# Cosine attention and a two-layer network: two and a half more group products by seven half-size products, another order of loads, one list of all operations

## The chip, the core and the metric

The kernel runs on one core of a Trainium2 chip. The core has engines with instruction queues of their own, each worked in order: TensorE (PE, with its weight loads PEld), VectorE (DVE), ScalarE (ACT), GpSimd (POOL), and SyncE (SP), which here issues nearly all DMA transfers. Matrix products are written into PSUM, eight banks of 128 partitions with 512 float32 each; operands lie in SBUF. The metric is the device time of one execution in microseconds. Before the change it is 274.62 us (median of 3 runs, 274.36 to 274.9).

## The reference

```python
batch, n_heads, seq, head_dim = (8, 8, 576, 64)          # q, k, v
theta = np.pi / 2.0 * pos / S
def phi(x, c, s):
    r = np.maximum(x, 0.0)
    return np.concatenate([r * c, r * s], axis=-1)       # 64 -> 128 features
q_p, k_p = phi(q, cos_w, sin_w), phi(k, cos_w, sin_w)
kv = np.einsum('bhsf,bhsd->bhfd', k_p, v)
z = np.sum(k_p, axis=2)
num = np.einsum('bhsf,bhfd->bhsd', q_p, kv)
den = np.einsum('bhsf,bhf->bhs', q_p, z)[..., None] + 1e-06
x = (num / den)                      # tokens 8 * 576 = 4608, d_model 8 * 64 = 512
h = x @ w_in                         # 512 -> 2048
g = np.maximum(0.01 * h, h)
out = g @ w_out                      # 2048 -> 512
```

Linear attention with cosine weights, for each batch and head, and then a two-layer network over all tokens. Nearly all the arithmetic is in the two products with `w_in` (called FFN1 here) and `w_out` (FFN2).

## The kernel before, in words

The tokens are worked in nine groups of 512: group g below 8 is the first 512 tokens of batch g, and group 8 is the last 64 tokens of all eight batches. For each batch the stages are these.

- Loads of q, k and v (float32) into stage buffers, and their preparation: `q_prep` and `k_token` (or `k_pair` for the first two batches) write relu(x) times the cosine and sine columns as float16, `v_pairs` casts v and leaves a column of ones beside it, which makes the sum z.
- `kv_sum`: 72 small matmuls over the keys of a batch, the key sum, copied by ACT into `kv`.
- q is transposed, by TensorE (`q_transpose`) for the first two batches and by DMA afterwards. `num` multiplies it with kv into PSUM, `divide` (three DVE instructions: add, reciprocal, multiply) writes x, and x is transposed into xT: by TensorE for groups 0 to 2, by DMA from group 3 on.
- FFN1 of the group: w_in has 16 tiles of 128 columns ("f-tiles", m) and 4 chunks of 128 rows (c). As whole products this is 16 x 4 matmuls of 512 token columns (`ffn1`), each pair of f-tiles followed by one ACT activation over 1024 columns into g.
- FFN2 of the group: 4 token tiles x 16 f-tiles, matmuls of 512 columns (`ffn2_mm`), or by seven products.

"By seven half-size products" means that a product of two matrices cut into 2 x 2 quarters is made of seven products of quarters (or of sums of quarters) instead of eight. For FFN1, `ffn1s` makes it in four units u with seven products n, each of four matmuls of 256 columns; `ffn1e` does what lies between: three copies in or out of PSUM (`b`, `s`, `u`), two additions (`y`, `z`), four half-size activations (`a`, `c`, `e`, `d`). The sums of quarters are made once for the weights (`w1_sum`) and once per group for x (`x_sum`). For FFN2, `ffn2s` makes the seven products, `weight_sum` the sums of the weights, `g_sum` those of g, and three partial results t1, t2, t3 and four results (`result`) follow on ACT and DVE.

In the kernel before, FFN1 is made whole for groups 0, 1 and 2 and by seven from group 3 on (`F7 = 3`, line 53); FFN2 is made whole for group 0 and by seven from group 1 on (`G7 = 1`, line 52).

The order of the work is written out by hand up to line 1014: the loads in lines 174 to 187 and 905 to 917, the attention of the first two batches, FFN1 of group 0, FFN2 of group 0 woven with the preparation of batch 1, and the first half of FFN1 of group 1. From there on the table `TUNE` (line 1020) gives the order of TensorE's units (strings in `O`) and, for every other operation, a place among them and an engine; `weave` merges the two. Each engine's queue gets its instructions in the order in which Python issues them; the dependences between engines become semaphore waits. `idle` matmuls (lines 194 to 199 and later) on a blank tile stand at places in the start where TensorE waits for data.

Stage buffers: four rotating ones, and beside them `ext` and `wext`, which hold chunks of w_in, of the fourth quarter of w_out, of v of batch 1 and of k of batches 1 and 3, until the sums of the seven products need that space.

## Time and profile before

| | |
|---|---|
| median of 3 runs | 274.62 us (274.36 to 274.9) |
| profiled execution, first to last instruction | 273.1 us |
| TensorE busy | 265.3 us |
| VectorE, ScalarE, GpSimd busy | 204.8, 179.2, 130.3 us |
| bytes moved by DMA | 57.07 MB |
| granted TensorE clock | 1.00 in every stretch |

The profile is of one execution; the page gives its own time as the span of 273.1 us from the first to the last instruction, 1.5 us less than the median of the runs. Two views of it, and how they are read. The page cuts the span into 40 slices of 6.83 us; a digit is the busy share of an engine in a slice, in tenths:

```profile
PE   8899999999999999999999999999999999999993
DVE  4850596677876796996989798897789957757852
ACT  7756547577985878898778776776744575565500
POOL 2586002992779456998695879742330004000000
DMA  6999999999899899869999996794565051111214
```

The groups of instructions have a line of the kernel, an engine, an operation, output and input with their shapes and a count; then the busy time and the mean duration of one in ns, and the idle time of that engine just before them with what ended it. A group of matmuls has a mean that is longer than the distance from one to the next, because matmuls are pipelined; the distance is read from a chain or a timeline, as length divided by count.

### The profile page before, as it was taken

How to read it: one execution, taken by the hardware profiler on the slowest of the kernel's cores; microseconds unless marked ns; L12 is line 12 of the kernel's file. 1: busy time of each engine (PE TensorE's matmuls, PEld its weight loads, DVE VectorE, ACT ScalarE, POOL GpSimd, SP SyncE). 2: the span in 40 equal slices, each digit the busy share in tenths (PEclk: the TensorE clock that was granted, in tenths of full speed). 3: DMA queues.
4: the chain of work that ended last, by engine and by line, in shares of the span. 5: the costliest groups of instructions: out<-in, count | busy, mean ns of one | idle time of the engine just before them, and what ended most of it. 6: DMA issues, size and time to landing. Idle time of an engine off the chain costs nothing.

```text
span 273.1 us, 7061 instructions
## 1 busy us (share of the span) xinstructions
PE 265.3 (97%) x2877; PEld 218.6 (80%) x2877; DVE 204.8 (75%) x419; ACT 179.2 (66%) x311; POOL 130.3 (48%) x104
## 2 busy tenths in 40 slices
PE   8899999999999999999999999999999999999993
PEld 3575555556885589999999999899999899999983
DVE  4850596677876796996989798897789957757852
ACT  7756547577985878898778776776744575565500
POOL 2586002992779456998695879742330004000000
PEclk9999999999999999999999999999999999999999
DMA  6999999999899899869999996794565051111214
GB/s 212 382 392 411 382 399 371 374 278 253 247 191 320 205 186 353 265 120 264 208 238 206 244 388 105 125 211 93 119 154 118 2 115 65 54 41 35 83 38 116
DMA packets 75120, 57.07 MB, mean 209 GB/s; under 512 B 47312, under 2 KB 63696, under 8 KB 74704
## 3 DMA queue, kind: packets, MB, share of 16 engines
q1 hardware_dynamic: 74480, 56.11, 74.6%
q10 hardware_dynamic: 608, 0.52, 0.6%
q8 instruction: 22, 0.36, 0.5%
q14 instruction: 10, 0.08, 0.1%
HBM read 36.70 MB, written 9.44 MB: 169 GB/s over the span
## 4 chain that ended last, share of the span: by engine, by line
PE 90%; DMA 3%; DVE 2%; POOL 1%; SPq 1%; issue 1%; ACT 1%; DVEq 0%
PE ps L759 34%; PE ps_f L642 27%; PE ps_h L490 15%; PE ps_o L516 5%; PE ps_kv L330 4%; DMA kst<-in_k_dram 3%; PE ps_num L416 3%; PE ps_f L759 1%; POOL kp L257 1%; PE ps_qt L402 1%; PE ps_xth L468 1%; PE ps_x L393 0%; SPq L135 0%; ACT g L500 0%; SPq L121 0%
## 5 line engine op out<-in xcount | busy, mean ns | idle before, releaser
L759 PEld LDWEIGHTS <-g 128*128 128x128 f16 x640 | 61.8, 98 | 7.5 <-ACT g L500 0.6
L759 PE MATMUL ps<-w,g 128*128 128x256 f16 x496 | 65.3, 273 | 0.4 <-ACT g L500 0.4
L669 ACT ACTIVATE g<-ps_f 128x512 f16<-128x512 f32 x72 | 41.9, 597 | 20.0 <-PE ps_f L642 10.3
L490 PE MATMUL ps_h<-xT,w 128*128 128x512 f16 (+1 forms) x208 | 43.5, 363 | 0.1
L642 PEld LDWEIGHTS <-w 128*128 128x128 f16 x384 | 41.6, 114 | 1.1 <-issue 0.3
L642 PE MATMUL ps_f<-xT,w 128*128 128x256 f16 x288 | 42.1, 273 | 0.2 <-DVE u L265 0.2
L490 PEld LDWEIGHTS <-w 128*128 128x128 f16 x208 | 22.8, 114 | 16.4
L500 ACT ACTIVATE g<-ps_h 128x1024 f16<-128x1024 f32 x24 | 24.1, 1023 | 13.1 <-PE ps_h L490 13.1
L759 PE MATMUL ps<-T,ext 128*128 128x256 f16 x240 | 32.4, 273 | 0.0
L257 POOL TENSOR_SCALAR kp<-kst,cos_t 128x256 f16<-128x256 f32 (+1 forms) x23 | 29.8, 1302 | 5.2 <-DMA kst<-in_k_dram 3.2
L642 PEld LDWEIGHTS <-wext 128*128 128x128 f16 x288 | 31.2, 113 | 0.5
L759 PEld LDWEIGHTS <-ext 128*128 128x128 f16 x256 | 24.8, 98 | 2.5
L257 POOL TENSOR_SCALAR qp<-qst,cos_t 128x512 f16<-128x512 f32 (+1 forms) x10 | 19.5, 1951 | 9.1 <-DMA qst<-in_q_dram 5.0
L257 POOL TENSOR_SCALAR kp<-kst,sin_t 128x256 f16<-128x256 f32 x15 | 20.2, 1348 | 4.9 <-PE ps_kv L330 2.7
L642 PE MATMUL ps_f<-X,wext 128*128 128x256 f16 x144 | 21.5, 273 | 0.0
L542 DVE TENSOR_TENSOR osb<-ps,ext 128x512 f32<-128x512 f32 x23 | 15.8, 688 | 7.4 <-PE ps L759 6.3
L542 DVE TENSOR_TENSOR ps_f<-ps_f,u 128x512 f32<-128x512 f32 x24 | 16.6, 694 | 5.6 <-PE ps_f L642 3.3
L432 DVE TENSOR_TENSOR xs<-ps_num,rden 128x512 f16<-128x512 f32 x28 | 19.4, 691 | 1.0
L669 ACT ACTIVATE g<-y 128x512 f16<-128x512 f32 x24 | 15.2, 632 | 6.9 <-DVE y L542 6.6
L257 POOL TENSOR_SCALAR qp<-qst,sin_t 128x512 f16<-128x512 f32 (+1 forms) x10 | 19.5, 1951 | 0.0
L542 DVE TENSOR_TENSOR ext<-g 128x512 f16<-128x512 f16 (+1 forms) x24 | 13.8, 576 | 5.1 <-ACT g L500 3.5
L542 DVE TENSOR_TENSOR y<-ps_f,s 128x512 f32<-128x512 f32 x24 | 16.4, 683 | 1.4 <-PE ps_f L642 1.3
(120 smaller groups left out, 455.9 us busy)
## 6 DMA issues: line engine op xcount, KB each, us to landing
out_dram<-osb SPq DMA_DIRECT2D x32, 256.0 KB, 2.6
qst<-in_q_dram SPq DMA_DIRECT2D x7, 1024.0 KB, 9.1
kst<-in_k_dram SPq DMA_DIRECT2D x5, 1152.0 KB, 7.6
vst<-in_v_dram SPq DMA_DIRECT2D x5, 1152.0 KB, 9.5
w2st<-in_moe_w_out_dram SPq DMA_DIRECT2D x3, 1024.0 KB, 14.1
vst<-in_v_dram SPq DMA_DIRECT2D x4, 576.0 KB, 6.4
ext<-in_moe_w_in_dram SPq DMA_DIRECT2D x4, 512.0 KB, 10.1
kst<-in_k_dram SPq DMA_DIRECT2D x2, 576.0 KB, 7.3
```

Source lines behind the costliest of these rows:

```text
L257: eng.tensor_scalar(out=o, in0=i, scalar1=0.0, scalar2=col, op0=ALU.max, op1=ALU.mult)
L330: nc.tensor.matmul(ps[:, o, (c - lo) * NE : (c - lo + 1) * NE], lhsT=st["kp", b][sl, c, j, :], rhs=vm[sl, c, j, :], start=(j == 0), stop=( ...
L402: nc.tensor.transpose(ps[:, h, :], qp[:, h, :], ident)
L416: nc.tensor.matmul(ps[lo:hi, h // 4, (h % 4) * NE : (h % 4 + 1) * NE], lhsT=qpT[:, h, lo:hi], rhs=kv[b][:, h, :],)
L432: nc.vector.tensor_tensor(out=xs, in0=ps[:, :, 0 : 4 * NE].rearrange("p a (b e) -> p a b e", e=NE)[:, :, :, 0:D], in1=rden.rearrange("p (a ...
L490: nc.tensor.matmul(ps[:, m % 2, lo:hi], lhsT=w1[m // 4, c][0][:, w1[m // 4, c][1], m % 4 : 512 : 4], rhs=xT[:, lo // P : hi // P, c, :], s ...
L500: nc.scalar.activation(st["g", g][:, m - 1 : m + 1, :], ps, AF.Lrelu)
L516: nc.tensor.matmul(st["ps_o", g, tt], lhsT=st["g", g][:, m, tt * P : (tt + 1) * P], rhs=w2[:, m, :], start=(m == 0), stop=(m == NFT - 1),)
L542: eng.tensor_tensor(out=o, in0=a, in1=b, op=op)
L642: nc.tensor.matmul(ps[:, mi * HT : (mi + 1) * HT], lhsT=a[:, c, 2 * r0 + mi : 512 : 4], rhs=b[:, c], start=(n in (1, 5) and mi == 0 and c ...
L669: nc.scalar.activation(st["g", g][:, m : m + 2, r * HT : (r + 1) * HT], {"a": A, "c": y22, "e": E, "d": B_}[e].rearrange("p (m t) -> p m t ...
L759: nc.tensor.matmul(ps[:, tt], lhsT=a[:, i, tt * P : (tt + 1) * P], rhs=b[:, i], start=(first and i == 0), stop=(i == NPR - 1 and (apart or ...
```

## The change

Three things change, and the code is rewritten around them.

1. FFN1 of groups 1 and 2 is made by seven products too (group 0 stays whole), and of FFN2 of group 0 the second eight f-tiles: its first eight are 4 x 8 matmuls of 512 columns (`E`), copied into the output tile `osb` (`ec`); the second eight are half of the seven products (`F0.n.tt.1`, four matmuls each). Their results are added to what lies in `osb` (`r0.n`), and so are t3, t1 and t2 (`d0.5`, `d0.4`, `d0.3`).
2. The loads come in another order. In the start: the first half of k, the second and then the first half of q, the second half of k, the first half of v, one chunk of w_in, the second half of v, the other chunks, with the first half of k of batch 1 ahead of the last of them. Then w_out's first quarter, q of batch 1, w_out's second quarter, the rest of k and all of v of batch 1, and only then w_out's second half, followed by batch 2. Stage buffers are four, given in turn by a table (`where`); `ext` and `wext` take w_in's chunks only.
3. All operations, loads, transposes, stores and idle matmuls among them, stand in one list `ORDER`, an item for each, with its engine after a colon (D, A or P). The program walks through the list and issues each. Places and engines are other ones throughout: among others 42 sums of g are on GpSimd, where all were on VectorE before. The idle matmuls are 25 instead of 29. PSUM is eight banks in four spaces, opened as pairs and split into single banks during the run (`split.h`, `split.n`, `join.n`).

The names in the list: `L` a load, `K` a key sum and `kv` its copy, `T` and `tc` a transpose of q and its copy, `Tq` and `Tx` DMA transposes, `N` numerators, `D` the divide, `X` and `xc` a transpose of x and its copy, `M` a matmul group of whole FFN1 and `a` its activation, `P` four matmuls of FFN1 by seven (group.unit.product), `F` four of FFN2 by seven (group.product.token tile.half), `Ws`, `Tw`, `Xs`, `S` sums of w_in, w_out, x and g, `t`, `r`, `st` partial results, results and stores.

```diff
-    G7 = 1
-    F7 = 3
+ORDER = """
+Lk0a setup blank:D kp0.1.c:D kp0.1.s:D Lq0b q0b.3.c:A Lq0a Lk0b kp0.0.s:D q0b.0.s:A kp0.0.c:D q0b.1.c:A
...
+v1.2:A k1b.5.c:P k1b.1.c:P N1a.1 k1b.0.c:D S0.1h:P E2.3 kp1.3.s:D D1a.0 E3.2 cw2.2.0:A cw2.2.1:A E3.3 D1a.1
+K1b kv1b:D X1a.0 X1a.1 xc1a.0:D E0.1 N1b.0 E0.2 xc1a.1:D N1b.1 ec2:A E0.3 E1.2 S0.2h:D ec3:A ec0:A E1.3 ec1:A
+D1b.1 split.n D1b.0 Lq2 X1b.1 xc1b.1:A Xs1.1:P Xs1.2:D P1.0.1 P1.1.1 X1b.0 b1.0:A xc1b.0:A P1.0.5 q2.1.c:D
...
+    where = {}
+    for n, key in enumerate(
+        [("q", 0), ("k", 0), ("v", 0), ("w1", 0), ("w2", 0), ("w2", 1), ("q", 1), ("k", 1), ("v", 1)]
+        + [("w2", 2), ("w2", 3)]
+        + [(nm, b) for b in range(2, B) for nm in "qkv"]
+        + [("qt", i) for i in range(J)]
+        + [("out", i) for i in range(J)]
+    ):
+        where[key] = stage[n % 4]
+    where["w1", 1] = wext
+    where["w1", 2], where["w1", 3] = ext[:, 0:NS], ext[:, NS:]
...
+    def ffn2(tt, lo, hi, eng):
+        for m in range(lo, hi):
+            nc.tensor.matmul(
+                bank[4 + tt],
+                lhsT=G[0][:, m, tt * P : (tt + 1) * P],
+                rhs=w2[:, m, :],
+                start=(m == 0),
+                stop=(m == NPR - 1),
+            )
...
+    for g in range(1, NG):
+        for u in range(4):
+            for n in range(1, 8):
+                op(f"P{g}.{u}.{n}", ffn1s, g, u, n)
+            for e in "bsuyz":
+                op(f"{e}{g}.{u}", between, g, u, e)
...
+    def ffn2s(g, n, tt, h, eng):
+        a, b = product(g, n)
+        ps = chain_ps(g, n, tt)
+        apart = g == LAST and CHAIN[n] == "Z"
+        first = n in FIRST or (g == LAST and n == 4)
+        at = 4 if g == 0 else 0
+        for i in range(4 * h, 4 * h + 4):
+            nc.tensor.matmul(
+                ps[:, tt],
+                lhsT=a[:, i, tt * P : (tt + 1) * P],
+                rhs=b[:, i],
+                start=(first and i == at and (apart or tt == 0)),
+                stop=(i == NPR - 1 and (apart or tt == 1)),
+                skip_group_check=True,
+            )
...
+    def result(g, n, t, eng):
+        o = first_quarter(n) if g == 0 else osb[:, (2, 5, 4, 3).index(n)]
+        if g == 0:
+            tt_op(o, half(flat(g, n)), o, ALU.add, eng)
+        elif t is None:
+            copy(o, flat(g, n), eng)
+        else:
+            tt_op(o, flat(g, n), t, ALU.add, eng)
...
+            if g == 0 and t is not None:
+                op(f"d{g}.{n}", tt_op, first_quarter(n), first_quarter(n), half(t), ALU.add)
+
+    op("split.h", change, ("h0", "h1"), 2)
+    op("split.n", change, ("n",), 2)
+    op("join.n", change, ("n",), 1)
+
+    engines = {"": None, "D": DVE, "A": ACT, "P": POOL}
+    for item in ORDER.split():
+        name, _, e = item.partition(":")
+        if name.startswith("idle"):
+            idle(*(int(x) for x in name.split(".")[1:3]))
             continue
+        OPS[name](engines[e])
```

More of the change, by code (lines that the diff above doesn't have):

```diff
@@ L20 @@
+"""
 @with_exitstack
@@ L398, in q_transpose @@
[L398 to L415 removed]
+            out=xT[g % 2].rearrange("p j c t -> p (j c) t"),
```

1432 lines of the change are left out of this document (564 added, 868 removed), and 17 rows, old and new, of the table TUNE.

## The prediction

> **What bounds the kernel now.** I read the page from the top: busy shares, slices, then the chain, then the waits of TensorE, then busy time by stretch.
>
> ```profile
> span 273.1 us, 7061 instructions
> PE 265.3 (97%) x2877; PEld 218.6 (80%) x2877; DVE 204.8 (75%) x419; ACT 179.2 (66%) x311; POOL 130.3 (48%) x104
> GB/s 212 382 392 411 382 399 371 374 278 253 247 191 320 205 186 353 265 120 264 208 238 206 244 388 105 125 211 93 119 154 118 2 115 65 54 41 35 83 38 116
> PE 90%; DMA 3%; DVE 2%; POOL 1%; SPq 1%; issue 1%; ACT 1%; DVEq 0%
> ```
>
> TensorE is busy 97% and holds 90% of the chain that ended last. A busy TensorE is not yet a TensorE without holes, because a pipelined matmul is drawn longer than its share; so the waits and the stretches come next (in a stretch: length, then busy us and instructions of PE, PEld, DVE, ACT, POOL, then clock, DMA share and GB/s).
>
> ```profile
> PE ps_numh L452 <- ACT kv L337: 0.7, 1, 0.7
> PE ps_kv L330 <- POOL vm L265: 0.4, 1, 0.4
> PE ps L759 <- ACT g L500: 0.4, 1, 0.4
> PE ps_x L393 <- ACT xT L263: 0.2, 1, 0.2
> PE ps_f L642 <- DVE u L265: 0.2, 1, 0.2
> ...
> 10.00:20.00 10.00, 8.54 (x152) 6.42 (x151) 7.43 (x18) 7.12 (x16) 7.51 (x9) 1.00 1.05 388
> 100.00:170.00 70.00, 70.00 (x890) 66.04 (x888) 59.45 (x130) 56.59 (x107) 57.52 (x39) 1.00 0.96 240
> 110.00:120.00 10.00, 10.00 (x111) 9.61 (x109) 9.30 (x23) 9.35 (x19) 10.00 (x6) 1.00 0.60 198
> 96.00:174.00 78.00, 77.82 (x958) 73.11 (x957) 67.39 (x144) 62.90 (x118) 62.72 (x43) 1.00 0.95 229
> 200.00:260.00 60.00, 60.00 (x598) 55.81 (x596) 45.96 (x86) 31.73 (x58) 5.90 (x5) 1.00 0.26 71
> ```
>
> After the start, TensorE waits visibly three times, 0.4 + 0.2 + 0.2 = 0.8 us; the granted clock is 1.00 throughout. The time is the sum of TensorE's work, a start in which data arrives, and a tail. So an edit is worth what it takes from TensorE's work, less what it makes TensorE wait. The other engines are near their own limit between 96 and 174 us (DVE 86%, ACT 81%, POOL 80%) and far from it after 200 us.
>
> **The change, part by part: TensorE's work.** Rows of the chain in order of time (start, length, what):
>
> ```profile
> 31.78 5.18 PE ps_o L516 x24
> 53.09 12.10 PE ps_h L490 x56
> 148.61 1.25 PE ps_kv L330 x72
> 174.96 3.49 PE ps L759 x32
> ```
>
> A 512-column matmul costs 5.18/24 = 0.216 us (12.10/56 gives the same), a 256-column one 3.49/32 = 0.109. A whole group product is 64 x 0.216 = 13.82 us; by seven half-size products it is 112 x 0.109 = 12.2 us, or 1.6 us less.
> - FFN1 of groups 1 and 2: 2 x 1.6 = 3.2 us less.
> - FFN2 of group 0, its second eight f-tiles: 32 x 0.216 = 6.91 becomes 56 x 0.109 = 6.10, 0.8 us less.
>
> Together 4.0 us. The transposes, the key sums and the numerators stay the same in kind and number. The warming matmuls go from 29 to 25, in places where TensorE waits for data: counted at nothing; if one of them delayed work it would cost 0.2 us.
>
> The Trainium skill ("TensorE: Matmul & The Clock Gate", section Back-to-back issue gap) gives 131 ns for a 512-column and 81 for a 128-column matmul in a stream with weight loads; between them my estimate for 256 columns is 98, and by it seven products would cost more than eight and the sum would be 6 us worse instead of 4 better. The rows of 216 and 109 ns disagree, and they decide.
>
> **Added elementwise work.** Mean ns of one stands after the busy time:
>
> ```profile
> L669 ACT ACTIVATE g<-ps_f 128x512 f16<-128x512 f32 x72 | 41.9, 597 | 20.0 <-PE ps_f L642 10.3 <-DVE ps_f L542 9.6
> L500 ACT ACTIVATE g<-ps_h 128x1024 f16<-128x1024 f32 x24 | 24.1, 1023 | 13.1 <-PE ps_h L490 13.1
> L263 ACT COPY ps_f<-ps_f 128x512 f32<-128x512 f32 x22 | 12.7, 577 | 4.0 <-PE ps_f L642 2.4 <-issue 1.2
> L542 DVE TENSOR_TENSOR y<-ps_f,s 128x512 f32<-128x512 f32 x24 | 16.4, 683 | 1.4 <-PE ps_f L642 1.3
> L542 DVE TENSOR_TENSOR X<-xT,X 128x512 f16<-128x512 f16 x6 | 2.5, 412 | 0.0
> L542 DVE TENSOR_TENSOR w<-w,w 128x1024 f16<-128x1024 f16 x1 | 0.7, 681 | 0.0
> L542 POOL TENSOR_TENSOR w<-w,w 128x1024 f16<-128x1024 f16 x1 | 2.1, 2123 | 0.0
> ```
>
> For each of the two groups: 12 copies (b, s, u) x 0.58 = 7.0, 8 additions (y, z) x 0.68 = 5.4, 16 half activations for 8 whole ones (16 x 0.597 - 8 x 1.023 = 1.4), 4 sums of x x 0.41 = 1.6; 15.4 us, so 31 for both. Group 0 gets three t, four results and three d at about 0.68 = 6.8, and four sums of g at 0.68 = 2.7. About 40 us of DVE and ACT work is new, all of it between the first product of group 1 and the numerators of group 4. Elsewhere some 40 sums of g go from DVE to POOL, each 2.12 instead of 0.68 us; POOL was busy 5.90 of 60 us after 200, so I price that at 0, with 0 to 1.4 us once if one such sum ends last.
>
> Whether the 40 us are hidden is the main question. In the new list, from P1.0.1 to D4.3, TensorE has 73 P and 58 F groups of four matmuls (131 x 0.437 = 57.2 us), three key sums (3 x 1.25), 12 numerators (8 matmuls each, 0.26 us until the next begins) and 5 transposes (0.23): 57.2 + 3.75 + 3.1 + 1.1 = 65.1 us.
>
> ```profile
> 78.54 0.39 PE L393 MATMUL ps_x<-ident,xs 128*128 128x128 f16 x4
> 78.77 0.60 PE L759 MATMUL ps<-ext,g 128*128 128x256 f16 x4
> ...
> 156.37 0.42 PE L416 MATMUL ps_num<-kv,qpT 128*128 128x66 f16 x8
> 156.63 0.60 PE L642 MATMUL ps_f<-X,wext 128*128 128x256 f16 x4
> ```
>
> In the same stretch the list has 141 DVE instructions (a divide is three), 120 on ACT and 43 on POOL. At the means of the stretch 100 to 170 us (59.45/130 = 0.457, 56.59/107 = 0.529, 57.52/39 = 1.475 us) that is 64.4, 63.5 and 63.4 us: 98% of all three engines, if TensorE never waits. The bounds: 0, since the list's place is not its time and an operation may run late without harm; and the 86% of DVE in the stretch 96 to 174, where 64.4/0.864 = 74.5 would mean 9.4 us of waiting. Nearest is the row 110 to 120, where the three were busy 28.65 of 30 us (95.5%) and TensorE did not wait: 191.3/3/0.955 = 66.8, less 65.1 gives 1.7 us of new waiting. I take 1.7, and since the old 0.8 us of waits lies in work that is replaced, 0.9 net.
>
> **The loads.** All loads, DMA transposes and stores are issued by SP in order, and the list changes that order. The GB/s of the slices (6.83 us each) add up to 1.45 MB at 6.8 us, 4.06 at 13.7, 6.73 at 20.5, 9.54 at 27.3, 12.15 at 34.1, 14.9 at 41.
>
> ```profile
> 15.22 2.15 POOL L265 CAST w<-w1st 128x512 f16<-128x512 f32 x3
> 15.32 0.74 PE L330 MATMUL ps_kv<-vm,kp 64*128 64x66 f16 x36 [0.36 <-POOL vm L265]
> 16.79 0.88 PE L490 MATMUL ps_h<-xT,w 128*128 128x256 f16 x6
> 43.66 0.69 POOL L265 CAST vm<-ext 128x576 f16<-128x576 f32 x1 [18.10 <-DMA ext<-in_v_dram]
> 43.86 0.74 PE L330 MATMUL ps_kv<-vm,kp 64*128 64x66 f16 x36
> ```
>
> - The start. The second half of the keys comes 0.59 MB sooner (0.59/0.38 = 1.5 us), the second half of v 0.26 MB later (0.7 us). The w_in chunk that FFN1 needs second is the 4.98th MB instead of the 3.93th, 1.05/0.39 = 2.7 us later. Before, the cast of these chunks began at 15.22 and the matmuls on them at 16.79; then at about 18.4 TensorE starts the rest, having by then all numerators behind it, which the old kernel has only at 18. Net between -1 and +2; I take +0.3.
> - The second batch. Its first half of v is complete after 12.5 MB instead of 13.5, about 35 us. In the old kernel the last part of v (15.2 MB, 41.8 us) was waited for until 43.66, so landing and issue add 1.9 us: 36.9, plus the cast 0.67, 37.6. By TensorE's work the new list reaches that key sum near 37. I take +0.4, between 0 and 1.5. What is late next: w_out's second half, but its first products (F0) stand behind some 20 P products of 0.437 us, 9 us after the first P.
> - The third and later batches use four stage buffers alone, each load behind the casts that free it; SP's queue holds the DMA transposes behind such a load. The list puts every load a batch ahead; 0, and up to 1 us if a transpose stands behind a waiting load.
>
> **The tail.** The last four products and additions keep their form, and six stores stand on each queue as before:
>
> ```profile
> 268.88 0.42 DVE L542 TENSOR_TENSOR osb<-ps_f,ext 128x256 f32<-128x256 f32 x1 [0.45 <-PE ps_f L759]
> ```
>
> The last addition begins at 268.88 and the span ends 3.8 us after that one. I take 0, between -0.5 and +0.7 (the last sum of g now stands only two product groups ahead of its product).
>
> **The sum.** -4.0 + 0.9 + 0.3 + 0.4 = -2.4 us. The profiled execution spans 273.1 us, 1.5 below the median of 274.62 (the part outside the span); 273.1 - 2.4 = 270.7, and with the same 1.5 us about 272.2.
>
> **The rivals.**
> 1. Everything is hidden: no new waits and the old 0.8 us gone, 274.62 - 4.8 = 269.8. For it speaks the row 110 to 120; against it that the stretch is 65 us long, not 10.
> 2. The other side: DVE, ACT and POOL become the bound between P1.0.1 and D4.3. At DVE's 86.4% of the stretch 96 to 174 TensorE waits 9.4 us, and 274.62 - 4.0 - 0.8 + 9.4 = 279.2; at 90% 6.5 us and 276.3. It decides from 4.8 us of waiting, that is below 93% of DVE. For it speaks that no stretch of the trace as long holds such a load, and that POOL's operations stretch beside a busy DVE (the same operation took 1.44 us at 59.62, in the fence below, and 1.13 at 76.05); against it that the list may have room that counts by place don't show.
> 3. The loads: the start loses 2 us and the second batch 1.5: 274.62 - 4.0 + 0.9 + 3.5 = 275.0.
> 4. The seven products save less, because weight loads set the pace: 112 x 0.114 (the weight load of FFN1) = 12.77, 1.05 a product, 2.6 us instead of 4.0, 273.6. Against it: the same lines run at 0.109 now.
>
> ```profile
> 59.62 1.44 POOL L257 TENSOR_SCALAR kp<-kst,sin_t 128x256 f16<-128x256 f32 x1
> 76.05 1.13 POOL L257 TENSOR_SCALAR kp<-wext,sin_t 128x256 f16<-128x256 f32 x1
> L642 PEld LDWEIGHTS <-w 128*128 128x128 f16 x384 | 41.6, 114 | 1.1 <-issue 0.3
> ```
>
> By the Trainium skill ("GPSIMD Engine Reference", section 8, Key points) GpSimd shares its memory interfaces with VectorE, so that both lose when they run together; these two rows agree, and it is a reason for rival 2.
>
> **How the numbers follow.** A measurement of this kernel tells 0.2% (0.5 us) from no change. Forecast (0.45): 270.8 to 273.8, always faster. Rival 1 (0.22): faster. Rival 2 (0.19): slower but for a tenth of it. Rival 3 (0.11): half faster, a fifth the same, the rest slower. Rival 4 (0.03): faster. So faster about 0.75, the same 0.05, slower 0.20. The range runs from just under rival 1, 269.3, to the 90% case of rival 2, 276.3; it leaves out about 1 in 20 below and 3 in 20 above.
>
> **What would show it.**
>
> ```profile
> L490 PE MATMUL ps_h<-xT,w 128*128 128x512 f16 x176 | 39.5, 379 | 0.1
> L516 PE MATMUL ps_o<-w,g 128*128 128x512 f16 x64 | 15.3, 379 | 0.0
> ```
>
> In the new profile TensorE's busy time should fall by about 4 us, FFN1's matmuls of 512 columns should fall from 176 to 48, FFN2's from 64 to 32, and those of seven-product form grow by 224 and 56. Waits of TensorE on DVE, ACT or POOL between some 43 and 110 us should add up to 1 to 3 us: none means rival 1, over 5 rival 2. The first matmuls of FFN1 show the start, the first key sum of the second batch the loads. I am wrong if TensorE's work does not fall by 4 us, or if the start moves by more than 2.

## The result, and the profile after

The changed kernel takes 300.9 us (median of 4 runs, 300.36 to 305.05) against 274.5 us before on the same chip: a ratio of 1.095, 95% interval 1.093 to 1.097. One execution, the one of 305.05 us, ran in a slower state; without it the median is 300.6 us, and the times of the experiments leave out such executions too. The changed kernel is slower by 26 us, outside the predicted range of 269.3 to 276.3, and on the other side. The profiled execution spans 298.5 us, against 273.1 before.

The page of the changed kernel: the span, the busy time of the engines, two rows of the 40 slices (7.46 us each) and the chain by engine.

```profile
span 298.5 us, 7440 instructions
PE 267.5 (90%) x2993; PEld 231.0 (77%) x2993; DVE 245.6 (82%) x448; ACT 182.3 (61%) x334; POOL 195.9 (66%) x141
DVE  4958999999989999997998889887978786586743
POOL 3825977899671885975994599787846514656400
PE 50%; DVE 24%; DMA 17%; issue 5%; SPq 1%; ACT 1%; DVEq 0%; ACTq 0%
```

TensorE holds 50% of the chain where it held 90%. VectorE is busy 41 us longer and GpSimd 66, ScalarE 3. The slices of VectorE show 9 nearly throughout from the fifth to the twentieth (30 to 149 us).

The longest waits of TensorE in the changed kernel (total, times, longest):

```profile
PE o L631 <- DVE w L244: 4.3, 1, 4.3
PE o L795 <- DVE ext L238: 3.0, 2, 2.0
PE o L795 <- DVE osb L238: 2.7, 2, 1.4
PE n L505 <- DVE xs L529: 2.5, 3, 1.4
```

The ones before added up to 0.8 us after the start; these are nearly all on VectorE. Now three stretches, first of the kernel before, then of the changed one (length, busy us of PE, PEld, DVE, ACT, POOL, clock, DMA share, GB/s):

```profile
60.00:80.00 20.00, 19.41 (x246) 15.05 (x246) 15.93 (x37) 17.16 (x29) 12.43 (x11) 1.00 1.04 228
80.00:100.00 20.00, 20.00 (x205) 13.00 (x206) 14.52 (x30) 14.13 (x18) 11.86 (x7) 1.00 0.92 237
140.00:160.00 20.00, 20.00 (x268) 18.76 (x266) 17.25 (x39) 16.72 (x31) 13.83 (x9) 1.00 1.02 229
```

```profile
60.00:80.00 20.00, 16.02 (x208) 14.15 (x207) 20.00 (x31) 16.06 (x33) 17.38 (x10) 1.00 0.85 206
80.00:100.00 20.00, 16.47 (x224) 14.05 (x222) 17.95 (x40) 12.98 (x26) 11.77 (x10) 0.91 0.81 220
140.00:160.00 20.00, 15.80 (x162) 14.21 (x161) 18.88 (x29) 12.12 (x24) 20.00 (x15) 1.00 0.80 190
```

VectorE is full from 60 to 80, GpSimd from 140 to 160, and TensorE stands still for 3.5 to 4.2 us in each of the three.

**Did TensorE's work fall?** Its busy time rose, from 265.3 to 267.5 us, but busy time counts a matmul in its drawn length, and after every wait the first one is drawn in full. Count times distance tells it better. Distances in an undisturbed place of the changed kernel:

```profile
111.38 0.60 PE L706 MATMUL h<-xT,w 128*128 128x256 f16 x4
111.81 0.60 PE L706 MATMUL h<-X,w 128*128 128x256 f16 x4
...
112.70 0.60 PE L795 MATMUL o<-w,g 128*128 128x256 f16 x4
```

Twelve matmuls in 1.32 us are 0.110 each, as before. The matmuls of 512 columns fell from 176 to 48 (FFN1) and from 64 to 32 (FFN2), those of 256 columns in seven-product form rose by 224 and 56. So 280 x 0.109 - 160 x 0.216 = -4.0 us: this step held exactly.

**Where the time went.** I gave every matmul that is no warming one its distance (0.216 us for 512 columns, 0.109 for 256, 0.056 for 128, 0.024 for 66, the last a mean: 1.25/72 = 0.017 in a key sum, 0.26/8 = 0.033 in a numerator) and added up what TensorE had begun by a given time. The whole is 254.0 us of work before and 250.0 after. All rows below "changed" are experiments, told further down: "no copies" is the changed kernel without the copies and additions of groups 1 and 2, the other indented rows start from the kernel with the sums on VectorE.

```
us of the span          20    40    60    80   100   120   140   160   200   240   last matmul
before                 7.5  27.5  46.9  65.9  86.1 106.1 126.3 146.4 185.9 225.5   268.6
changed                6.5  20.6  37.8  53.4  67.8  87.2 105.1 119.8 158.2 197.6   293.3
  no copies            5.1  19.9  38.2  55.9  74.2  93.1 109.8 125.6 164.3 203.2   287.5
sums on VectorE        6.4  22.3  39.2  54.5  74.1  92.3 109.0 126.5 165.5 204.3   286.7
  no w_in sums         5.7  25.2  41.7  57.3  77.1  94.3 112.4 132.0 170.7 209.8   281.3
  no preps on VectorE  5.0  22.1  39.4  56.8  76.9  94.8 108.5 127.4 166.0 205.0   286.0
  no preps at all      6.2  22.6  40.7  58.9  79.3  97.9 110.5 130.7 170.4 209.3   281.6
  no loads             5.8  23.1  40.2  55.4  73.2  91.3 109.0 128.4 167.7 206.6   284.8
```

The changed kernel is 6.9 us of work behind by 40 us, 12.5 by 80, 18.3 by 100, 26.6 by 160, and no more than 28 from then on. So the loss is all ahead of 160 us, and it has several places.

### The profile page after: what moved, and what is told of

Read it like the earlier page. It is cut to its first block, busy times and chain, and to the rows that moved or that the text cites. A ratio compares the mean times of both kernels' runs of the same rounds, so it can differ in the third digit from the quotient of the medians.

```text
span 298.5 us, 7440 instructions
## 1 busy us (share of the span) xinstructions
PE 267.5 (90%) x2993; PEld 231.0 (77%) x2993; DVE 245.6 (82%) x448; ACT 182.3 (61%) x334; POOL 195.9 (66%) x141
## 4 chain that ended last, share of the span: by engine, by line
PE 50%; DVE 24%; DMA 17%; issue 5%; SPq 1%; ACT 1%; DVEq 0%; ACTq 0%
PE o L795 21%; PE h L706 20%; DMA qpT<-qp 6%; DMA wext<-in_moe_w_in_dram 4%; DVE ext L238 4%; DMA stage<-in_k_dram 3%; DVE kp L408 3%; DMA stage<-in_moe_w_in_dram 3%; DVE kp L250 3%; DVE qp L250 2%; DMA xT<-xs 2%; PE n L505 2%; DVE T L238 2%; DVE y L238 2%; PE o L631 1%
## 5 line engine op out<-in xcount | busy, mean ns | idle before, releaser
L726 ACT ACTIVATE g<-h 128x512 f16<-128x512 f32 x90 | 52.7, 597 | 32.5 <-DVE h L238 15.1
L795 PE MATMUL o<-w,g 128*128 128x256 f16 x504 | 68.1, 276 | 1.3 <-DVE osb L238 1.3
L706 PEld LDWEIGHTS <-w 128*128 128x128 f16 x512 | 55.5, 114 | 6.4 <-issue 4.3
L706 PE MATMUL h<-xT,w 128*128 128x256 f16 x356 | 51.2, 273 | 1.8 <-DVE u L244 1.2
L795 PE MATMUL o<-T,ext 128*128 128x256 f16 x232 | 33.0, 275 | 4.4 <-DVE ext L238 3.0
L250 POOL TENSOR_SCALAR kp<-stage,cos_t 128x256 f16<-128x256 f32 (+1 forms) x18 | 20.8, 1158 | 13.9 <-PE n L432 10.8
L706 PE MATMUL h<-X,wext 128*128 128x256 f16 x180 | 26.0, 273 | 1.8 <-DVE h L244 0.9
L238 POOL TENSOR_TENSOR g<-g 128x512 f16<-128x512 f16 (+1 forms) x14 | 23.7, 1693 | 5.8 <-DVE ext L238 5.8
L238 DVE TENSOR_TENSOR h<-h,u 128x512 f32<-128x512 f32 x31 | 21.5, 693 | 4.7 <-PE h L706 1.9
L250 POOL TENSOR_SCALAR qp<-stage,cos_t 128x512 f16<-128x512 f32 (+1 forms) x11 | 23.2, 2114 | 1.9 <-DMA qpT<-qp 1.8
L529 DVE TENSOR_TENSOR xs<-n,rden 128x512 f16<-128x512 f32 x30 | 20.7, 692 | 1.0
```

Source lines behind the costliest of these rows:

```text
L238: eng.tensor_tensor(out=o, in0=a, in1=b, op=how)
L250: eng.tensor_scalar(out=o, in0=i, scalar1=0.0, scalar2=col, op0=ALU.max, op1=ALU.mult)
L529: nc.vector.tensor_tensor(out=o, in0=ps[:, :, 0 : 4 * NE].rearrange("p a (b e) -> p a b e", e=NE)[:, :, :, 0:D], in1=r.rearrange("p (a b) ...
L706: nc.tensor.matmul(ps[:, mi * HT : (mi + 1) * HT], lhsT=a[:, c, 2 * r0 + mi : 512 : 4], rhs=b[:, c], start=(n in (1, 5) and mi == 0 and c ...
L726: nc.scalar.activation(G[g % 2][:, m : m + 2, r * HT : (r + 1) * HT], {"a": A, "c": y22, "e": E, "d": B_}[e].rearrange("p (m t) -> p m t", ...
L795: nc.tensor.matmul(ps[:, tt], lhsT=a[:, i, tt * P : (tt + 1) * P], rhs=b[:, i], start=(first and i == at and (apart or tt == 0)), stop=(i ...
```

## The experiments

The first theory was that a two-input sum on GpSimd and an instruction of VectorE with two operands in SBUF run one after the other. What pointed to it, in the timeline of the changed kernel (start, length, engine):

```profile
59.52 0.69 DVE L238 TENSOR_TENSOR g<-g 128x1024 f16<-128x1024 f16 x1
60.12 2.62 DVE L238 TENSOR_TENSOR T<-w,T 128x1024 f16<-128x1024 f16 x1
...
59.75 2.44 POOL L238 TENSOR_TENSOR w<-w 128x1024 f16<-128x1024 f16 x1 [0.90 <-ACT g L726]
```

The sum on GpSimd runs from 59.75 to 62.19. A sum of VectorE of the same size, which began inside it, takes 2.62 us instead of 0.69 and ends 0.55 us after it. The trace of the kernel before shows the same twice, once here, where GpSimd's sum ends at 204.13 and VectorE's 0.55 us later:

```profile
203.49 1.18 DVE L542 TENSOR_TENSOR ext<-g 128x1024 f16<-128x1024 f16 x1
...
202.97 1.16 POOL L542 TENSOR_TENSOR xT<-xT 128x512 f16<-128x512 f16 x1
```

Over all runs here there are 20 places where a VectorE sum over 1024 float16 columns begins inside a two-input float16 sum of GpSimd; in each it ends 0.55 us after that one. The Trainium skill says ("SBUF — State Buffer", section Who interferes with whom) that a VectorE instruction with two SBUF inputs contends with a GpSimd instruction that reads SBUF, and that the lock on the ports that they share is exclusive. The traces agree for these sums and are narrower for others: beside GpSimd's preparations, which read float32, 34 of 41 such sums kept their 0.67 to 0.69 us (in the kernel before, the changed one and the next one). The changed kernel has 61 two-input sums on GpSimd.

### Sums to VectorE, and sums in one-input form

```diff
-Ws0.2:P Ws1.1:P S0.1h:P Xs1.1:P Tw3.1:P S0.4h:P d0.3:P ...
+Ws0.2:D Ws1.1:D S0.1h:D Xs1.1:D Tw3.1:D S0.4h:D d0.3:D ...
```

> The changed kernel with all 61 two-input sums that stand on GpSimd (S, Xs, Ws, Tw, d0.3) given to VectorE at the same places. Theory (a two-input sum on GpSimd and a VectorE instruction that reads two SBUF operands, or one through both read sides, run one after the other, so that a 0.68 us sum on VectorE took 2.62 at 60.12 us): stretched VectorE instructions vanish, VectorE gains 61 x 0.6 = 35 us of work and loses about as much stretch, so its busy time stays near 245 us, but no wait is longer than an instruction: 275 to 285 us. Rival A (VectorE, ScalarE and GpSimd are simply short of time between 43 and 110 us): more work on VectorE makes it slower than 300.9. Rival B (order of the loads): no change, 299 to 302.

Measured: 293.3 us (292.48 to 296.4), ratio to before 1.071 (1.065 to 1.077). The means of two shapes on VectorE, first in the changed kernel, then in this one:

```profile
L250 DVE TENSOR_SCALAR kp<-stage,cos_t 128x256 f16<-128x256 f32 x21 | 12.9, 629 | 1.0 <-DMA stage<-in_k_dram 1.0
L238 DVE TENSOR_TENSOR T<-w,T 128x1024 f16<-128x1024 f16 x2 | 3.7, 1855 | 0.0
```

```profile
L243 DVE TENSOR_SCALAR kp<-stage,cos_t 128x256 f16<-128x256 f32 x21 | 8.5, 412 | 0.0
L231 DVE TENSOR_TENSOR T<-w,T 128x1024 f16<-128x1024 f16 x2 | 1.4, 682 | 0.0
```

VectorE did 61 instructions more and was busy 247.1 us instead of 245.6: in the changed kernel it lost nearly as much to blocking as these sums cost it here. Against 300.6 us, 7.3 came back; the mechanism is there, and its size missed the expected 275 to 285. Some 3 of the 7.3 us are TensorE's clock: in the changed kernel it was halved from 37.7 to 41.1 and from 85.5 to 88.9 us, where 3.3 us of work began that took twice its time; here it was not halved before the end.

```diff
         if eng is POOL:
+            for i in (a, b):
+                POOL.tensor_scalar(out=o, in0=i, scalar1=1.0, scalar2=0.0, op0=ALU.mult, op1=ALU.add)
+            return
```

> The changed kernel, but each of the 61 two-input sums on GpSimd is replaced by two one-input instructions of about half its length (a copy by multiply and add of each operand in turn), so that GpSimd stays about as busy at the same places; the sums are left out of the computation by this (the output keeps only the second operand). Theory: VectorE's stretched instructions return to 0.4 to 0.75 us and the time falls to 270 to 280 us. Rival A (GpSimd's lateness or load is the cause): 295 us or more. Rival B (order of the loads): 299 to 302.

Measured: 291.7 us (289.64 and 293.79), ratio 1.063 (1.054 to 1.072), 8.8 us less than the changed kernel. GpSimd is as busy as there (195 us) and in one-input form; the sums themselves are left out, so the output isn't the reference's. The expected 270 to 280 was missed, and VectorE's sums did not return to 0.75 us. The sum shown above, at its place in this run:

```profile
61.87 1.53 DVE L237 TENSOR_TENSOR T<-w,T 128x1024 f16<-128x1024 f16 x1
...
61.51 1.35 POOL L233 TENSOR_SCALAR w<-w 128x1024 f16<-128x1024 f16 x1 [0.91 <-ACT g L725]
```

So one input is no cure: this instruction of GpSimd, which reads float16, holds the sum up too, until 0.54 us after its end. It is only shorter, 1.35 us instead of 2.44. What the run shows is that these 8.8 us are not the price of GpSimd's busy time. That the shorter blocking gives the 8.8 us fits VectorE's busy time, 235.4 us instead of 245.6, but nothing isolates it.

### The sums on GpSimd, in the kernel before

```diff
+    ON_POOL, moved = {1: 2, 2: 4, 3: 7, 4: 3, 5: 7, 6: 7, 7: 6, 8: 4}, {}
...
+        moved[g] = moved.get(g, 0) + 1
+        eng = POOL if moved[g] <= ON_POOL.get(g, 0) else DVE
-            tt_op(S1[:, sl], a21, a22, ALU.add)
+            tt_op(S1[:, sl], a21, a22, ALU.add, eng)
...
```

> The kernel before, with 40 of its sums of g (2, 4, 7, 3, 7, 7, 6, 4 in groups 1 to 8) given to GpSimd at the same places, nothing else changed: the load order and the whole products of FFN1 stay. Theory: VectorE instructions beside them stretch by up to 2 us each and TensorE waits: 285 us or more. Rival A (shortage of time in the early stretch alone): VectorE is relieved by 40 x 0.6 us and the time stays within 274 to 278. Rival B (loads): 274 to 276.

Measured: 316.6 us, ratio 1.154 (1.152 to 1.155). TensorE's waits:

```profile
PE ps_kv L330 <- POOL kp L257: 9.9, 5, 4.6
PE ps_f L642 <- DVE X1b L542: 7.2, 1, 7.2
PE ps L763 <- POOL ext L542: 5.6, 2, 3.3
```

Forty sums moved to GpSimd cost 42 us where nothing else changed. Key preparations that stood behind the sums on GpSimd's queue are late for the key sum, the sums are late for their products, and VectorE's sums of x are held up. The waits also cost clock, which is the third column from the end in this row:

```profile
109.60:119.80 10.20, 5.60 (x27) 3.89 (x27) 8.85 (x11) 2.31 (x5) 9.84 (x8) 0.50 0.50 169
```

It was halved in six stretches, 30.7 us together, in which 12.6 us of work began; at half the clock that took 12.6 us more. So of the 42 us some 12 to 13 are the clock and the rest waiting. The prediction had priced a move of this size at 0 to 1.4 us. Why the new list bears it better is not shown.

### Exchanging work, and using ScalarE

```diff
-Ws0.2:P ... (the 61 sums) ... q2.0.c:D k2.7.s:D ... (33 preparations)
+Ws0.2:D ... (the 61 sums) ... q2.0.c:P k2.7.s:P ... (33 preparations)
```

> As the run with all sums on VectorE, and in exchange 33 one-input preparations of k and q of later batches move from VectorE to GpSimd at their places (1.13 and 1.99 us each, no more than the time that the sums freed). Theory: VectorE's busy time falls to about 235 us, TensorE's waits to a few us: 268 to 276 us, and the 4 us of saved product work become visible if the waits stay under 4. Rival A: 285 or more. Rival B: 299 or more.

Measured: 304.9 us, ratio 1.111 (1.109 to 1.113), worse by 11.6 than with the sums alone on VectorE. VectorE fell to 237.8 us, but the key sums now wait 7.4 us for GpSimd, and 5.3 us of work began at half the clock. Then ScalarE, which has some 110 us to spare:

```diff
-Ws0.2:P ... cw2.0.1:P cw2.0.0:D q1.0.s:D q1.2.c:D kv1a:A xc1a.0:D q2.1.c:D ... (the 61 sums, and 163 others)
+Ws0.2:D ... cw2.0.1:A cw2.0.0:P q1.0.s:A q1.2.c:A kv1a:D xc1a.0:A q2.1.c:A ... (places unchanged)
```

> The changed kernel with its list in the same order, and another choice of engines: the 61 two-input sums that ran on GpSimd run on VectorE, and the copies inside the new products (b, s, u), the preparations of keys and queries, the casts of v, cw2, xc, tc and kv are spread so that by the durations of the old trace VectorE has some 220 us, ScalarE some 190 and GpSimd some 75. Theory (too much elementwise work was put on VectorE and on GpSimd, and none on ScalarE): 272 to 285 us, VectorE below 82% busy, and the waits of TensorE on VectorE and GpSimd under half of those of the changed kernel. Rival (the order of the list, or the new products themselves, are late whatever engine does the work): stays within 8 us of the 293.3 us of the kernel with the sums on VectorE.

Measured: 308.0 us, ratio 1.120 (1.117 to 1.123). In the stretch from 118 to 142 us:

```profile
ACT kp L241 <- DMA stage<-in_k_dram: 4.9, 1, 4.9
PEld L788 <- ACT g L719: 3.5, 1, 3.5
```

A key preparation that now heads ScalarE's queue waits 4.9 us for its load, and the relus behind it, which have their data, wait with it; TensorE then waits for the relus. VectorE had 18 us less to do than with the sums on it, and the time was 14.7 us worse; 10.6 us of work began at half the clock, so most of the 14.7 is the clock after the waits. Exchanging engines at fixed places puts instructions that wait for a load ahead of others that could run.

### One cast, and the order of the loads

```diff
-cw2.0.0:D
+cw2.0.0:A
```

> The changed kernel with one cast, the first part of w_out (cw2.0.0), on ScalarE instead of VectorE. Theory (TensorE's wait of 4.3 us at the first E product is for that cast, which stands behind key preparations of VectorE that GpSimd's sums stretch): the first E product begins 2 to 4 us sooner, TensorE's 4.3 us are gone, and the end comes 1 to 5 us sooner, 296 to 300. Rival (the loads set the start): E1.0 stays within 1 us and the end within 1 us of 300.9.

Measured: 300.35 us, ratio 1.094 (1.092 to 1.096). The wait only changed its name:

```profile
29.19 1.04 ACT L235 CAST w<-stage 128x1024 f16<-128x1024 f32 x1 [4.78 <-DMA stage<-in_moe_w_out_dram]
30.14 1.93 ACT L610 ACTIVATE g<-h 128x1024 f16<-128x1024 f32 x2
...
31.21 1.74 PE L601 MATMUL h<-xT,w 128*128 128x512 f16 x4 [3.90 <-ACT g L610]
```

On ScalarE the cast waits for its load until 29.19, and two relus wait behind it; on VectorE it waits behind key preparations. Neither theory had this.

```diff
-Lk1b ... Lv1a ... Lv1b ... Lw2.2 ... Lw2.3
+Lw2.2 Lw2.3 Lk1b ... Lv1a ... Lv1b
```

> The changed kernel with the two loads of w_out's second half moved back ahead of the second half of the second batch's k and v in the list. Rival (load order is what costs the time): at least 5 us less than 300.9. Theory (elementwise work): within 4 us of 300.9, in either direction.

Here the last quarter of w_out overwrites the buffer of batch 1's q before it is prepared, so the values differ from the reference's, and the preparation of q now waits for that load:

```profile
42.58 0.48 DVE L243 TENSOR_SCALAR qp<-stage,sin_t 128x512 f16<-128x512 f32 x1 [6.21 <-DMA stage<-in_moe_w_out_dram]
```

Measured: 302.7 us, ratio 1.103 (1.098 to 1.108). TensorE waits 5.0 us for this preparation, a wait that the edit itself made. So the run does not test the order of the loads in the start, and no other run does. By 60 us this run has 5.4 us less of TensorE's work done than the changed kernel, and by 200 us 2.4: later stretches take a part of a loss in the start back.

### Leaving work out

```diff
-b1.0:A s1.0:A u1.0:A y1.0:D z1.0:D ... (40 items of groups 1 and 2)
...
```

> The changed kernel with the 40 copies and additions between the half-size products of groups 1 and 2 (b, s, u, y, z) left out; the relu of the third quarter then reads PSUM directly, and the products themselves stay, so the output of these two groups isn't the reference's. Theory (the added elementwise work, not TensorE's new order, costs the time): at least 8 us less than the 300.9 us of the changed kernel, 280 to 292. Rival (the load order, or the sums on GpSimd alone): within 4 us of 300.9.

Measured: 294.4 us (291.09 to 295.1), ratio 1.069 (1.062 to 1.076). 6.2 us, less than the 8 expected and more than the rival's 4. By the prediction's prices these 40 items are 25 of its 40 us of new elementwise work.

The next runs start from the kernel with the sums on VectorE (293.3).

```diff
-Ws0.1:D Ws0.2:D Ws1.1:D Ws1.2:D Ws1.4:D Ws0.4:D Ws0.3:D Ws1.3:D
...
```

> The kernel with the sums on VectorE (293.3 us), and the eight sums of w_in blocks (Ws) left out, 8 x 0.69 = 5.5 us of VectorE between 24 and 42 us; the products that read them read a plain block of w_in instead, so the output isn't the reference's. The kernel before makes these sums at 80 to 97 us. Theory (brought forward, they hold up the casts and key preparations that the first products of w_out and the second batch wait for): the first E product begins before 33.5 us instead of 35.2, and the end comes 3 to 6 us sooner, 287 to 290. Rival (the start is late because of its loads): within 1.5 us of 293.3.

Measured: 289.7 us, ratio 1.055 (1.052 to 1.058). This met its expectation. Six of these sums stand at 80 to 97 us in the kernel before. In the changed list, whose group 1 needs them from about 51 us on, they stand at 24 to 41, where VectorE also casts weights and prepares the keys of batch 1. By 40 us TensorE has done 25.2 us of work here, against 22.3 with the sums and 27.5 in the kernel before: 2.9 of the 5.2 us that the start loses.

```diff
-q2.1.c:D q2.2.s:D q2.0.c:D k2.7.s:D ... (56 preparations, batches 2 to 7)
```

> The kernel with the sums on VectorE (293.3 us), and the 56 preparations of keys and queries of batches 2 and on that stand on VectorE left out, some 28 us of its time; the tiles keep older values, so the output isn't the reference's. Theory (VectorE's load of 92 to 97% between 45 and 170 us is what makes TensorE wait there): VectorE about 75% there, 275 to 283 us. Rival (the order of the list is late by itself): 288 or more.

Measured: 292.0 us, ratio 1.061 (1.056 to 1.066): no difference that the intervals show, where 275 to 283 was expected. VectorE's share between 45 and 175 us fell from 94% to 82%, what it was in the kernel before (first row: this run, second: the kernel with the sums on VectorE):

```profile
45.00:175.00 130.00, 117.84 (x1489) 106.53 (x1488) 106.70 (x212) 96.62 (x185) 65.50 (x48) 0.99 0.97 246
```

```profile
45.00:175.00 130.00, 117.35 (x1481) 105.38 (x1482) 121.76 (x259) 95.60 (x185) 65.39 (x45) 1.00 0.94 245
```

So VectorE's load is not, by itself, the rest. The table shows that this run is 2.8 us ahead of its base by 100 us and has lost it again by 140: TensorE waited 3.3 us for a DMA transpose of x, until 132.7, and had half its clock from 134.4 to 137.8.

Both omissions together:

```diff
-Ws0.1:D ... Ws1.3:D   (8 sums)
-q2.1.c:D q2.2.s:D ... (56 preparations)
```

> Both omissions together: the sums on VectorE, the eight sums of w_in and the 56 preparations on VectorE left out; the output isn't the reference's. Theory: 269 to 279 us, TensorE idle under 16 us of the span. Rival (the order of the list): over 284.

Measured: 290.6 us, ratio 1.058 (1.051 to 1.064). Missed; the two omissions together give no more than the sums of w_in alone.

```diff
         done.add(("kp", b, j, f, lo))
         need(("kin", b))
-        phi_half(
+        for _ in range(2 if b > 1 and eng is not ACT and eng is not POOL else 1):
+            phi_half(
...
```

> The kernel before, with each preparation of keys and queries of batches 2 and on that stands on VectorE done twice, which changes no value: some 20 us more VectorE work between 45 and 170 us, which brings it from 79% to about 92% there, the load of the changed kernel with its sums on VectorE. Theory (that load is what TensorE waits for): 282 to 296 us. Rival (the old order has room for it, and the new order is what is late): 274 to 278.

Measured: 288.8 us (285.35 to 288.89), ratio 1.048 (1.043 to 1.054). 20.4 us more on VectorE (225.2 instead of 204.8) cost the old kernel 14 us, with 1.9 us of work begun at half the clock. Its largest wait is one that it did not have:

```profile
PE ps_kv L331 <- DVE kp L257: 4.1, 5, 2.3
```

So at these places the old order had little room on VectorE, with a share of 82% between 45 and 175 us.

### Transposes and loads

With VectorE relieved, TensorE's longest wait was 3.3 us for a DMA transpose of x, issued by SyncE behind a load. I moved eight items on SyncE's queue:

```diff
-Lv3a Tq3.0   Lk4 ... Tq3.1   Lq5 Tq4.0 Tx3   Lk5 ... Tq4.1   Lq6 ... Tq5.0   Lk6 ... st1.4 ... Tx4   Lv6 ... Tq5.1
+Tq3.0 Lv3a   Tq3.1 Lk4   Tq4.0 Tx3 Lq5   Tq4.1 Lk5   Tq5.0 Lq6   Tx4 st1.4 Lk6   Tq5.1 Lv6
```

> The kernel with the sums on VectorE (293.3 us), with eight items on SyncE's queue moved by a few places: the DMA transposes of groups 3 to 6 (Tq3.0, Tq3.1, Tx3, Tq4.1, Tq5.0, Tx4, Tq5.1) are issued ahead of the bulk loads (and one store) that stood right before them; everything else as it was. Theory (a transpose right behind a load of 1.1 MB takes 4.5 to 8 us where it takes 1.7 to 2 us in the kernel before, and what follows it on SyncE is late): transposes of x at most 3 us, and 2 to 6 us sooner, 287 to 291. Rival (transposes are hidden while VectorE paces the stretch): within 1.5 us of 293.3.

Measured: 296.3 us, ratio 1.078 (1.072 to 1.084). A transpose of x on SyncE's queue, and a wait of TensorE:

```profile
102.13 1.81 SPq L489 DMA_TRANSPOSE xT<-xs  x1
...
133.42 0.60 PE L699 MATMUL h<-xT,w 128*128 128x256 f16 x4 [2.20 <-ACT g L719]
```

The transpose got short, 1.81 instead of 2.99 us, and no time was gained. The loads came later, and with them the preparations; in this stretch ScalarE waits for loads, and TensorE for a relu behind that.

The same moves without the 56 preparations:

```diff
-q2.1.c:D q2.2.s:D ... (56 preparations)
+the eight moves
```

> The same moves on the kernel that leaves out the 56 preparations of VectorE (292.0 us; output not the reference's for the same reason). Theory (with VectorE relieved the transposes are what TensorE waits for between 100 and 140 us, 3.3 us for one of x and 1.2 for one of q): TensorE's waits on transposes below 1 us, 4 to 10 us sooner, 282 to 288. Rival (something else in the order): 290 or more.

Measured: 294.2 us, ratio 1.071 (1.067 to 1.075). TensorE no longer waits for transposes, and nothing is gained: the loads are late instead, and its new waits are for key preparations of GpSimd and for relus.

And without the sums of w_in:

```diff
-Ws0.1:D ... Ws1.3:D   (8 sums)
-q2.1.c:D q2.2.s:D ... (56 preparations)
+the eight moves
```

> The same moves on the kernel that leaves out the preparations and the eight sums of w_in (290.6 us). Theory (sums on GpSimd, VectorE's load, the early sums and the transposes are together all that is lost): 276 to 284 us. Rival (the new order is late for another reason too): 287 or more.

Measured: 292.5 us, ratio 1.063 (1.057 to 1.069). Missed. The theory that four causes add up falls here.

With all work done, and three sums later:

```diff
-Ws1.1:D ... Ws1.2:D ... Ws1.4:D ... E1.0 ... Ws1.3:D ... P1.0.1 ... Xs1.3:D
+E1.0 ... Ws1.3:D ... P1.0.1 ... Xs1.3:D Ws1.1:D Ws1.2:D Ws1.4:D
```

> The kernel with the sums on VectorE and the transposes moved, and three sums of w_in that only the third and fourth unit of group 1 need (Ws1.1, Ws1.2, Ws1.4) behind the first P products instead of ahead of the first E product; all work is done. Theory (2.1 us less VectorE work ahead of the cast that the first E product waits for): 1 to 3 us less than the kernel with the transposes moved alone. Rival (the later stretch is paced by VectorE and gives nothing back): within 1 us of it.

Measured: 297.7 us, ratio 1.082 (1.080 to 1.085). In this list Ws1.3, which overwrites a block of w_in, stands ahead of the moved sums, so they are sums of a changed block and the output isn't the reference's. The start gained (24.7 us of work by 40 instead of 22.9), and by 80 us it was given back (55.5 against 56.0).

The last two take away all the elementwise work of later batches' inputs, or all their loads:

```diff
-176 items k2..k7, q2..q8, v2..v7 on all engines
```

> The kernel with the sums on VectorE (293.3 us), and all 176 preparations of q and k and casts of v of batches 2 and on left out, on every engine (about 28 us of VectorE, 37 of ScalarE, 74 of GpSimd); loads, transposes, stores and all products stay, so the output isn't the reference's. Theory (the three elementwise engines and the loads that wait for their buffers are what TensorE waits for after the start, and the order of TensorE's work is sound): 268 to 278 us. Rival (the order of the list, or the transposes, are late by themselves): 285 or more.

Measured: 289.7 us, ratio 1.056 (1.051 to 1.061), where theory had 268 to 278. The waits between 50 and 120 us are nearly gone (79.3 us of work by 100, against 74.1), and then, on SyncE's queue and TensorE:

```profile
118.49 0.46 SPq L263 DMA_DIRECT2D stage<-in_k_dram  x1
119.74 7.57 SPq L476 DMA_TRANSPOSE xT<-xs  x1
...
130.95 1.04 PE L686 MATMUL h<-xT,w 128*128 128x256 f16 x4 [5.16 <-DMA xT<-xs]
131.79 1.06 PE L775 MATMUL o<-ext,g 128*128 128x256 f16 x4
```

and in this stretch, with the granted clock as the third column from the end:

```profile
128.70:135.30 6.60, 3.79 (x18) 2.53 (x19) 4.27 (x8) 0.12 (x1) 0.00 (x0) 0.50 1.04 273
```

The transpose of x is issued 1.25 us after a load of 1.15 MB, with a store between them, and takes 7.57 us. TensorE waits 5.16, and its clock is halved for 6.8 us (128.5 to 135.3), 4.3 of them after the wait: four matmuls begin in 0.84 us instead of 0.44. Between 120 and 140 this run does 12.6 us of work, less than the changed kernel (17.9).

```diff
-Lq2 Lk2 Lq3 Lv2 Lk3 Lq4 Lv3b Lv3a Lk4 Lv4 Lq5 Lk5 Lv5 Lq6 Lk6 Lv6 Lq7 Lv7 Lk7
```

> The kernel with the sums on VectorE (293.3 us), and the 19 loads of q, k and v of batches 2 to 7 left out; the preparations work on what lies in the buffers, so the output isn't the reference's. Theory (the elementwise engines are late, not the data): 287 to 293 us. Rival (loads a batch ahead through four stage buffers, and transposes that share the queue with them, are late): 283 or less.

Measured: 292.4 us, ratio 1.066 (1.064 to 1.068). The same transpose without the load ahead of it:

```profile
127.16 1.81 SPq L488 DMA_TRANSPOSE xT<-xs  x1
```

and two stretches, with VectorE as the third busy time:

```profile
60.00:80.00 20.00, 15.95 (x210) 13.75 (x209) 19.86 (x45) 16.95 (x33) 8.39 (x5) 1.00 0.26 67
80.00:100.00 20.00, 18.24 (x266) 16.80 (x264) 19.20 (x43) 15.86 (x33) 13.50 (x12) 1.00 0.52 94
```

The transposes of x take 1.7 to 2.2 us, TensorE waits for none, VectorE is 96 to 99% busy in these stretches, and nearly all of TensorE's waits are for it. The two runs together say what each alone could not: behind the start, two things are late side by side, elementwise work on queues that are full, and transposes behind loads. Whoever takes one away meets the other. Both taken away at once was not run.

## Why the prediction was wrong

- **TensorE's work, -4.0 us: right.** The counts are as forecast and the distances 0.109 and 0.216 us hold.
- **That TensorE's busy time would fall by 4 us: wrong** as a reading. It rose by 2.2, since matmuls after a wait are drawn in full, and since the clock was halved for two stretches of 3.4 us, the first after a wait of 4.3 us, the second after three that add up to 3.5. That cost some 3 us and stands in no term of the sum; with the sums on VectorE it doesn't happen. The Trainium skill ("TensorE: Matmul & The Clock Gate", section What's actually happening) gives the clock as halved after at least one idle window of about 3.4 us. The length of the stretches agrees, 3.4 us or a multiple; the wait can be shorter: without the copies of groups 1 and 2, one of 2.3 us (17.6 to 19.9) was followed by half the clock from 21.2 to 24.6, while with the sums on VectorE one of 2.45 was not.
- **"Some 40 sums of g go from DVE to POOL ... I price that at 0, with 0 to 1.4 us once": wrong.** It costs 7.3 us in the new list (with the sums of w_in, x and w_out that also stood there), and 42 us in the old one, the halved clock included. I compared duration with spare time on GpSimd (2.12 us each, 5.90 of 60 busy) and saw neither that a sum blocks VectorE while it runs nor what stands behind it on GpSimd's queue. Both were to be asked of the profile: it had the sum of 1.18 us at 203.49, and the text itself quoted the rule of the shared interfaces, as a reason for rival 2, and gave it no price.
- **"Added elementwise work", 0.9 us net: the step that failed.** I took the price from a 10 us row in which three engines were 95.5% busy and TensorE didn't wait, and spread it over 65 us. Leaving 25 of the 40 us out of the changed kernel gave 6.2 us back, where the term for all of it is 0.9. Doubling some preparations in the old kernel shows a price of the same kind: 20.4 us more on VectorE cost 14. A share over all engines says how much work there is and not whether each piece ends before its reader. The list gave ScalarE 3 us of the new work and VectorE and GpSimd the rest, which counts by engine over the whole kernel would have shown; in the stretch I had found all three at 98%.
- **The sums of w_in were counted at nothing**, because they are made before and after. They move from 80 to 97 us to 24 to 41 us, and leaving them out there gave 3.5 us back. That is not the same as making them later: three of them moved back by some places gained nothing. A step brought forward is an added step for the stretch that it arrives in.
- **The start, +0.3: wrong.** TensorE is 6.9 us of work behind by 40 us, not at most 2; 5.2 with the sums on VectorE, 2.3 without the early sums. I had weighed only megabytes, and the first product of w_out waited for a cast on VectorE. What the new order of the loads did to the start is not tested. Part of the loss in the start is given back later: after 5.4 us less by 60 us, one run ended 1.8 us later.
- **The second batch's loads, +0.4, and the later loads, 0 to 1: too small.** A transpose of x behind a load takes 2.8 to 7.6 us, those of the kernel before 1.3 to 2.0. With VectorE's load in place this hardly shows; with it gone, it is the next bound.
- **Rival 2**, an elementwise engine as the bound from the first product of group 1, with 0.19, named the right place and direction, and 276 to 279 us; the price was too small by 22. It was worked out as one engine's share in one stretch. TensorE waited 8.5 us between 43 and 110 us, more than the 5 that were to speak for it; but VectorE was 95% busy from the first product of group 1 on (the row below), above the 93% (by its own sum 64.4/69.9 = 92%) from which it should have cost nothing, in part because a blocked instruction counts as busy. The stretch in the changed kernel:

```profile
51.00:130.00 79.00, 68.71 (x851) 61.63 (x850) 74.74 (x144) 61.42 (x121) 61.05 (x42) 0.98 0.93 245
```

What stays open: of the 26 us, the runs settle 7.3 (sums on GpSimd, with the clock) and 3.5 (the early sums of w_in, left out). The 6.2 us of the copies and additions were measured with the sums still on GpSimd; how much of them is the same loss as the 7.3 was not run. The other 15, to which the 4 us not gained have to be added, are located by the table (2 to 3 us ahead of 40 us, the rest up to 160), but from 293.3 us no single omission gives more than 3.6 back, and beside the sums every exchange of engines or places cost time or gave nothing measurable. That VectorE's load and the transposes lie side by side rests on two runs and the stretch from 60 to 140 us; that they are all of it is only argued. No kernel run here beats the one before.

## What to carry to other kernels

Price added elementwise work by adding as much of it to the kernel at hand, in the same stretch, and not by the idle share of its engines: 20 us of it on an engine 82% busy cost 14. Look at the granted clock behind every new wait: it made some 12 of the 42 us that the sums on GpSimd cost the old kernel. Where work changes its engine, ask what it blocks while it runs and what stands behind it in order on the new queue, loads among it. And where taking away a suspected cause gives nothing back, look for the second limit beside it before dropping the first: only the opposite omission shows it.

## What the runs showed of the hardware

- A two-input sum on GpSimd (2.44 us for 128x1024 float16) holds up a two-operand float16 sum of VectorE that begins inside it until 0.55 us after its own end: 2.62 us instead of 0.69, and so in 20 of 20 places. A one-input instruction of GpSimd that reads float16 does the same (1.53 us beside one of 1.35). Most preparations, which read float32, did not (34 of 41).
- A DMA transpose of x took 1.7 to 2.2 us in the run without the later loads and up to 7.57 us behind a load of 1.15 MB on the same queue.
- TensorE's clock fell to 0.50 for 3.4 us or a multiple, up to 10.2, after waits of 2.3 to 7.2 us; not every wait of 2.4 us did it. At 0.50 a 256-column matmul took 0.21 us instead of 0.109 (four in 0.84).
